# Folding the squares of W_out with VectorE before the norm products, and squaring at the end of a step

## The chip, the cores and the metric

The kernel runs on one core of one Trainium2 chip. The metric is device time in microseconds (us) of one execution. Five engines work side by side, each through its own queue in order: TensorE (PE in the profile, with its weight loads as PEld), VectorE (DVE), ScalarE (ACT), GpSimd (POOL) and SyncE (SP, which here only issues DMAs).

## The reference

Attention over a pooled memory is followed by one feed-forward layer. `phi` is softmaxed over 32 memory slots and pools `k` and `v` into 32 rows per head; the queries attend to these rows; the heads side by side are the rows of `x` (4608 x 512).

```python
a = softmax(phi, axis=2)
k_m = einsum('bhsm,bhsd->bhmd', a, k); v_m = einsum('bhsm,bhsd->bhmd', a, v)
attn = softmax(q @ k_m.T / 8, axis=-1)
x = (attn @ v_m) as (4608, 512)
h = x @ w_in            # 512 x 2048
g = h - tanh(h)
out = g @ w_out         # 2048 x 512
```

## The kernel before, in words

**Precision and the check.** `w_in` and `w_out` come as float64. The fast path splits each into two float16 parts (`win_hi`, `win_lo`, `wout_hi`, `wout_lo`) and uses a polynomial for `h - tanh(h)`. This is right only if the sizes of the inputs lie in certain windows, so the kernel also measures these: per column of W_out, the sum of squares must lie in `WO_WIN`. All measurements go into the tile `stat`; `check` (word GG, L948) compares them on VectorE, `check_all` (GX, L964) sums the verdicts with one TensorE product `pgood`, and if the sum falls short a slow path (`wide_path`) recomputes everything. With the inputs used it does not run.

**The steady part.** The tokens are cut into 18 units of 256 (u = 0 to 17), W_in's columns into four blocks of 512 (fb = 0 to 3). One step is one pair (u, fb); a loop at L896 walks over them from u = 4, and the table `PLAN_C` counts them by slots, slot = 4u + fb. The profile's names don't hold the pair; the order listings below do (`g142` is u = 14, fb = 2, slot 58). A step does, in program order:

- `mm1` (L562): 24 to 48 products into the one PSUM tile `hs`, from the attention weights `ah`, `al` and the tiles `ph`; then ScalarE squares it, `u<-hs` (L579).
- `g1` (L584): VectorE `h<-hs,u` (L587). After it `hs` may be written by the next step.
- the first words of the plan, among them `P` (L529): products into the PSUM tile `pp`, read by ScalarE (L537) and by VectorE in `PL` (L542).
- `g1_square` (L590, ScalarE), `a_forms` (L614: four VectorE adds `f<-g`, L621, of the step before), `g2` (L594: VectorE `h<-u,h`, L597).
- `mm2_blocks` (L686): 48 products of the step two before into PSUM tiles `x` and `o`.
- `window_sum` (L442, ScalarE), the plan's words after ";", `g2_high` (L600: ScalarE `g<-h`, L603) and `g3` (L606: GpSimd `g<-h,g`, L608).
- words put off (`due`): CE and CQ load blocks of the float64 weights, CW squares one on GpSimd (`fy<-chk`, L439), SI and SO square a quarter of the weights on ScalarE; then `evict` (L761) where a unit ends; then the plan's words after "|".

**The norms.** `squares_out` (SO, L468) lets ScalarE square four blocks of W_out (128 x 2048, float16) into `sqo`, which lies in the one buffer `e`. `norms_out` (NO, L472) multiplies it with a column of ones on TensorE: for each of four column groups four products that add up in PSUM, 16 in all, into the tile `pno`; ScalarE copies the sums out, `wn<-pno` (L483), and after the last part VectorE adds the four parts into `stat` (L486). For W_in there are SI and NI likewise; there, for three of four parts, `squares_sum` (SS, L449) has VectorE fold the four blocks into one first (two float16 adds, L452 and L453), and NI needs four products.

**One PSUM buffer, `pa`,** serves `pp`, `pno`, `pni`, the scores `psc`, the transposes `ptr` and `pgood` in turn: each waits until the one before has been read out.

**The order** on every engine is that in which the code issues the instructions (`in_order`, L938); no scheduler moves anything.

Of the kernel before, what the change touches and what calls it, by code (L numbers as in the profile page):

```python
# [18 lines left out]
P = 128  # L19
# [20 lines left out]
CW = (  # L40
    0.33333331252017, -0.13333128520786, 0.053934788850892, -0.021660115374759,
    0.0082189218977914, -0.0025104593252184, 0.000420695493864,
)
# [2 lines left out]

V_WIN = (2.0 ** -12, 0.0025)
WI_WIN = (1.002 * 2.0 ** -6, 1.497)
WO_WIN = (2.0 ** -6, 3.5)
N_F1 = 32  # L50
N_ROWS = 2

# [285 lines left out]
def split_path(ctx, tc, c, ins, out):  # L338
    nc = tc.nc
# [95 lines left out]
    def window(k):  # L435

        hf = raws.pop(k).bitcast(F32).rearrange("p (f w) -> p f w", w=2)[:, :, 1]
        y = big.tile([P, 512], F32, tag="ot", name=f"fy{k}")
        nc.gpsimd.tensor_tensor(y, hf, hf, op=ALU.mult)  # L439
        return y, k  # L440

    def window_sum(y, k):  # L442
        nc.scalar.activation(y, y, AF.Relu, bias=c["one"], scale=-(2.0 ** 30), accum_out=stat[:, k : k + 1])
# [28 lines left out]
    def norms_out(part):  # L472
        if part == 0:
            acc["n"] = big.tile([P, 4, 4], F32, tag="wn", name="wn", bufs=1)
        sq = acc.pop(("q", part))
        pa = ps_a.tile([P, 2, 512], F32, tag="pa", name=f"pno{part}")
        for k in range(4):
            for i in range(4):
                nc.tensor.matmul(
                    pa[:, 0, k : k + 1], sq[:, i, P * k : P * k + P], c["ones16"],  # L480
                    start=(i == 0), stop=(i == 3),
                )
        nc.scalar.activation(acc["n"][:, :, part], pa[:, 0, 0:4], AF.Copy, scale=(S_W * S_Q) ** -2)  # L483
        if part == 3:
            o = N_CHECK - 4
            nc.vector.tensor_reduce(stat[:, o : o + 4], acc["n"], axis=AX.X, op=ALU.add)  # L486
# [75 lines left out]
    def mm1(u, fb):  # L562
        hp = acc["hp"] if "hp" in acc else ps_h.tile([P, 4, UT], F32, tag="h", name=f"h{u}{fb}")
        for k in range(4):
            cs = slice(P * k, P * k + P)
            for b, ta, tu, w in segs(u):
                d = st[b]
                ph, pl = d["p"][fb][0:2]
                n = 0
                for g in range(2):  # L570
                    for px, ax in ((ph, "ah"), (ph, "al"), (pl, "ah")):
                        nc.tensor.matmul(  # L572
                            hp[:, k, tu : tu + w], px[:, g, cs], d[ax][:, g, ta : ta + w],
                            start=(n == 0), stop=(n == 5),
                        )
                        n += 1
        yield
        uu = big.tile([P, 4, UT], F32, tag="us" if "hp" in acc else "uu", name=f"u{u}{fb}", bufs=1 if "hp" in acc else 2)
        nc.scalar.activation(uu, hp, AF.Square, scale=1.0 / (S_A * S_P))  # L579
        gs[u, fb] = (hp, uu)  # L580
# [3 lines left out]
    def g1(u, fb, stay=False):  # L584
        hp, uu = gs[u, fb]
        h3 = hp if stay else big.tile([P, 4, UT], F32, tag="h3", name=f"h3{u}{fb}")
        nc.vector.scalar_tensor_tensor(h3, hp, C2 * S_G / (S_A * S_P), uu, op0=ALU.mult, op1=ALU.mult)  # L587
        gs[u, fb] = (h3, uu)

    def g1_square(u, fb):  # L590
        uu = gs[u, fb][1]
        nc.scalar.activation(uu, uu, AF.Square, bias=c["beta"])  # L592

    def g2(u, fb, stay=False):  # L594
        hp, uu = gs[u, fb]
        h3 = big.tile([P, 4, UT], F32, tag="h3", name=f"h3{u}{fb}") if stay else hp
        nc.vector.scalar_tensor_tensor(h3, uu, CC, hp, op0=ALU.add, op1=ALU.mult)  # L597
        gs[u, fb] = (h3, uu)

    def g2_high(u, fb):  # L600
        h3 = gs[u, fb][0]
        gg = big.tile([P, 2, 4, UT], F16, tag="gg", name=f"g{u}{fb}", bufs=3)
        nc.scalar.activation(gg[:, 0], h3, AF.Copy)  # L603
        gs[u, fb] = (h3, gg)

    def g3(u, fb, eng):  # L606
        h3, gg = gs[u, fb]
        eng.tensor_tensor(gg[:, 1], h3, gg[:, 0], op=ALU.subtract)  # L608

    def a_block(gg, th, kh):  # L610

        return gg[:, :, 2 * kh : 2 * kh + 2, P * th : P * th + P]

    def a_forms(u, fb):  # L614

        gg = gs[u, fb][1]
        a11, a21, a12, a22 = (a_block(gg, th, kh) for kh in range(2) for th in range(2))
        f = big.tile([P, 2, 4, 2, P], F16, tag="uu", name=f"f{u}{fb}")
        s4, s3, s1, s2 = (f[:, :, i] for i in range(4))
        for o, x, y, op in ((s3, a21, a11, ALU.subtract), (s1, a21, a22, ALU.add), (s2, s3, a22, ALU.add), (s4, a12, s2, ALU.subtract)):  # L620
            nc.vector.tensor_tensor(o, x, y, op=op)  # L621
        gs[u, fb] = (f, gg)
# [207 lines left out]
    def go(word, whole=True):  # L830

        name = word.rstrip("0123456789")
        run = going.pop(word, None) or STEPS[name](*(int(x) for x in word[len(name):]))
        if run is None or not hasattr(run, "send"):
            return
        for _ in run:
            if not whole:
                going[word] = run
                return

    for word in START.split():
        if ":" in word:
            k, tag = word.split(":")
# [17 lines left out]
    PLAN_C = (  # L861
# [5 lines left out]
    )  # L867
    tasks = {}
    for b in range(3, B):
# [4 lines left out]
    loads, chk, due, squared = list(range(32)), [], [], []  # L874

    def borrow(tag):
        chk.append(loads.pop(0))
        load_raw(chk[-1], tag, "chk")

    def step(word, late=False):  # L880
        if word[0] == "C" or word[:2] in ("SI", "SO"):
            if not late:
                due.append(word)
            elif word == "CW":
                squared.append(window(chk.pop(0)))
            elif word[0] == "C":
                borrow({"E": "e", "Q": "q", "S": "sc"}[word[1]])
            else:
                go(word)
        else:  # L890
            go(word)
# [4 lines left out]
    for sl, (u, fb) in enumerate(slots, 18):  # L896
        if sl == 18:
            acc["x"] = ps_h.tile([P, 2, 512], F32, tag="h", name="x")
            acc["hp"] = ps_h.tile([P, 4, UT], F32, tag="h", name="hs")
        todo = ["", "", ""]  # L900
        for w in tasks.get(sl, []):
            w, _, todo_2 = w.partition("|")
            w, _, todo_1 = w.partition(";")
            for i, x in enumerate((w, todo_1, todo_2)):
                todo[i] += " " + x

        def do(i):
            for x in todo[i].split():
                step(x)

        list(mm1(u, fb))
        g1(u, fb)
        do(0)
        g1_square(u, fb)
        a_forms(*forms.pop())
        g2(u, fb)
        queue.append((u, fb))
        v, vb = queue.pop(0)
        mm2_blocks(v, vb, vb == 0, vb == NFB - 1)
        while squared:  # L920
            window_sum(*squared.pop(0))
        do(1)
        g2_high(u, fb)
        g3(u, fb, nc.gpsimd)
        while due:
            step(due.pop(0), True)
        evict()
        forms.append((u, fb))
        do(2)
    a_forms(*forms.pop())  # L930
    for u, fb in queue:
        mm2_blocks(u, fb, fb == 0, fb == NFB - 1)
# [15 lines left out]
def check(tc, c, big):  # L948
# [4 lines left out]
    o = N_F1  # L953
    for n, (lo, hi) in ((2 * B, V_WIN), (DF // P, WI_WIN), (DM // P, WO_WIN)):
        s, g = stat[:, o : o + n], good[:, o : o + n]
# [196 lines left out]
```

## Time and profile before

| what | us |
|---|---|
| median of 3 runs (lowest, highest) | 660.62 (660.04, 660.83) |
| the profiled execution's own time | 660.87 |
| its span from first to last instruction | 659.1 |
| PE busy | 641.5 (97%) |
| DVE busy | 522.7 (79%) |
| ACT busy | 375.7 (57%) |
| POOL busy | 251.0 (38%) |

A row of the timeline holds start, duration, engine, line, operation, output and inputs, shape, and the number of instructions taken together; in brackets how long the engine stood idle before it, and what ended that. The chain of waits follows the last instruction back, at each step to what released it or to the instruction before it on its engine. A busy PE is not PE at its peak.

### The profile page before, as it was taken

How to read it: one execution, taken by the hardware profiler on the slowest of the kernel's cores; microseconds unless marked ns; L12 is line 12 of the kernel's file. 1: busy time of each engine (PE TensorE's matmuls, PEld its weight loads, DVE VectorE, ACT ScalarE, POOL GpSimd, SP SyncE). 2: the span in 40 equal slices, each digit the busy share in tenths (PEclk: the TensorE clock that was granted, in tenths of full speed). 3: DMA queues.
4: the chain of work that ended last, by engine and by line, in shares of the span. 5: the costliest groups of instructions: out<-in, count | busy, mean ns of one | idle time of the engine just before them, and what ended most of it. 6: DMA issues, size and time to landing. Idle time of an engine off the chain costs nothing.

```text
span 659.1 us, 15599 instructions
## 1 busy us (share of the span) xinstructions
PE 641.5 (97%) x6690; PEld 455.5 (69%) x6690; DVE 522.7 (79%) x790; ACT 375.7 (57%) x509; POOL 251.0 (38%) x173
## 2 busy tenths in 40 slices
PE   8879999999999999999999999999999999999996
PEld 4355656566557777777776777777687777887785
DVE  6989999999855787875988679767977686867763
ACT  4567686666424456545655465545654577666541
POOL 0315141221222245442535253625452455455521
PEclk9999999999999999999999999999999999999999
DMA  8999245302423402333331524141505333234201
GB/s 342 375 377 393 96 169 184 114 2 65 145 96 102 145 20 74 113 101 133 105 114 65 168 66 153 60 142 66 163 25 195 101 100 125 61 109 142 77 33 37
DMA packets 25996, 84.98 MB, mean 129 GB/s; under 512 B 2880, under 2 KB 2880, under 8 KB 25152
## 3 DMA queue, kind: packets, MB, share of 16 engines
q1 hardware_dynamic: 24624, 81.55, 36.1%
q10 hardware_dynamic: 1296, 2.36, 0.9%
q8 instruction: 54, 0.88, 0.6%
q14 instruction: 22, 0.18, 0.1%
HBM read 72.37 MB, written 11.53 MB: 127 GB/s over the span
## 4 chain that ended last, share of the span: by engine, by line
PE 76%; DVE 12%; DMA 6%; issue 2%; ACT 2%; POOL 1%; SPq 0%; DVEq 0%; ACTq 0%
PE hs L572 20%; PE x L715 13%; PE o L708 12%; PE o L715 10%; PE o L651 6%; PE h L572 4%; DMA kv<-in_kva_dram 3%; PE o1h L651 3%; PE pp L524 3%; PE pkv L220 2%; DMA raw<-in_w_out_dram 2%; DVE h L587 2%; DVE wt L384 1%; DVE h L597 1%; PE psc L272 1%
## 5 line engine op out<-in xcount | busy, mean ns | idle before, releaser
L608 POOL TENSOR_TENSOR g<-h,g 128x1024 f16<-128x1024 f32 x64 | 138.5, 2165 | 329.2 <-ACT g L603 234.3
L572 PEld LDWEIGHTS <-ph 128*128 128x128 f16 x2304 | 176.7, 98 | 20.7 <-issue 6.0
L572 PE MATMUL hs<-ah,ph 128*128 128x256 f16 (+3 forms) x1152 | 151.5, 246 | 0.0
L587 DVE SCALAR_TENSOR_TENSOR h<-hs,u 128x1024 f32<-128x1024 f32 x54 | 65.9, 1220 | 91.3 <-ACT u L579 91.2
L603 ACT ACTIVATE g<-h 128x1024 f16<-128x1024 f32 x72 | 75.9, 1055 | 91.7 <-DVE h L597 89.5
L572 PE MATMUL hs<-al,ph 128*128 128x256 f16 (+3 forms) x576 | 127.6, 246 | 0.0
L592 ACT ACTIVATE u<-u,beta 128x1024 f32<-128x1024 f32 x72 | 82.4, 1147 | 55.1 <-DVE h L587 54.1
L708 PE MATMUL o<-wout_hi,g 128*128 128x512 f16 x432 | 104.7, 380 | 0.0
L715 PEld LDWEIGHTS <-f 128*128 128x128 f16 x896 | 87.5, 98 | 10.3
L597 DVE SCALAR_TENSOR_TENSOR h<-u,h 128x1024 f32<-128x1024 f32 x72 | 87.4, 1216 | 0.8 <-ACT u L592 0.7
L579 ACT ACTIVATE u<-hs 128x1024 f32<-128x1024 f32 x54 | 55.0, 1019 | 55.3 <-PE hs L572 50.8
L715 PE MATMUL x<-bt,f 128*128 128x256 f16 x672 | 82.5, 273 | 0.0
L715 PEld LDWEIGHTS <-g 128*128 128x128 f16 x672 | 64.1, 98 | 26.6 <-issue 5.0
L708 PEld LDWEIGHTS <-g 128*128 128x128 f16 x432 | 40.5, 98 | 44.0 <-issue 8.1
L651 PEld LDWEIGHTS <-g 128*128 128x128 f16 x384 | 36.6, 98 | 46.6 <-issue 3.4
L621 DVE TENSOR_TENSOR f<-g 128x512 f16<-128x512 f16 x112 | 64.9, 620 | 4.3 <-POOL g L608 3.4
L651 PE MATMUL o<-wout_hi,g 128*128 128x512 f16 x192 | 58.8, 380 | 0.0
L572 PE MATMUL h<-ah,ph 128*128 128x256 f16 (+3 forms) x384 | 49.6, 246 | 0.1
L572 PE MATMUL h<-al,ph 128*128 128x256 f16 (+2 forms) x192 | 42.4, 246 | 0.2 <-POOL al L515 0.2
L542 DVE SCALAR_TENSOR_TENSOR ph<-pp,ph 128x1024 f16<-128x1024 f32 x31 | 37.6, 1213 | 0.6 <-ACT ph L537 0.6
L537 ACT ACTIVATE ph<-pp 128x1024 f16<-128x1024 f32 x32 | 32.5, 1017 | 7.4 <-PE pp L524 7.4
L651 PE MATMUL o<-wout_lo,g 128*128 128x512 f16 x96 | 36.4, 379 | 0.0
(146 smaller groups left out, 979.1 us busy)
## 6 DMA issues: line engine op xcount, KB each, us to landing
kv<-in_kva_dram SPq DMA_DIRECT2D x20, 516.0 KB, 4.2
q<-in_qt_dram SPq DMA_DIRECT2D x16, 576.0 KB, 4.3
chk<-in_w_in_dram SPq DMA_DIRECT2D x16, 512.0 KB, 5.6
chk<-in_w_out_dram SPq DMA_DIRECT2D x16, 512.0 KB, 3.4
out_dram<-r SPq DMA_DIRECT2D x27, 256.0 KB, 2.4
kv<-in_kva_dram SPq DMA_DIRECT2D x6, 1032.0 KB, 9.0
raws<-in_w_in_dram SPq DMA_DIRECT2D x12, 512.0 KB, 7.2
raw<-in_w_out_dram SPq DMA_DIRECT2D x12, 512.0 KB, 6.6
```

The lines of the kernel that those rows point to most:

```text
L542: nc.vector.scalar_tensor_tensor(pl, pa, S_P / (S_V * S_W), ph, op0=ALU.mult, op1=ALU.subtract)
L572: nc.tensor.matmul(hp[:, k, tu : tu + w], px[:, g, cs], d[ax][:, g, ta : ta + w], start=(n == 0), stop=(n == 5),)
L579: nc.scalar.activation(uu, hp, AF.Square, scale=1.0 / (S_A * S_P))
L587: nc.vector.scalar_tensor_tensor(h3, hp, C2 * S_G / (S_A * S_P), uu, op0=ALU.mult, op1=ALU.mult)
L592: nc.scalar.activation(uu, uu, AF.Square, bias=c["beta"])
L597: nc.vector.scalar_tensor_tensor(h3, uu, CC, hp, op0=ALU.add, op1=ALU.mult)
L603: nc.scalar.activation(gg[:, 0], h3, AF.Copy)
L608: eng.tensor_tensor(gg[:, 1], h3, gg[:, 0], op=ALU.subtract)
L621: nc.vector.tensor_tensor(o, x, y, op=op)
L651: nc.tensor.matmul(o, gx[:, k, P * tt : P * tt + P], wx[:, 4 * fb + k, :], start=(first and k == 0 and wx is wout_hi and gx is gh), stop=( ...
L708: nc.tensor.matmul(o[th], gg[:, 0, k, P * th : P * th + P], wout_hi[:, 4 * fb + k, :], start=(first and k == 0), stop=False)
L715: nc.tensor.matmul(dst, a(1 - n, kk), b(n, kk), start=(new and kk == 0 and n == 0), stop=(end and kk == 1 and n == 1))
```

## The change

Between the squaring of a part of W_out and its norm products stands now a step word SS, that is, the two VectorE adds of `squares_sum`; `norms_out` makes four products in place of sixteen. The words move in the plan: SO0 stays at slot 56, SO1 to SO3 stand at 59, 61 and 63 (before 58, 60, 62), each right behind the NO of the part before it; NO0 to NO3 at 59, 61, 63 and 65 (before 57, 59, 61, 63); SS0 to SS3 at 58, 60, 62 and 64. And in every step the words SI and SO come after `evict` and after the words behind "|", instead of before both. The window of W_out's norms is a little narrower.

```diff
-WO_WIN = (2.0 ** -6, 3.5)
+WO_WIN = (1.002 * 2.0 ** -6, 3.493)
...
-            for i in range(4):
-                nc.tensor.matmul(
-                    pa[:, 0, k : k + 1], sq[:, i, P * k : P * k + P], c["ones16"],
-                    start=(i == 0), stop=(i == 3),
-                )
+            nc.tensor.matmul(pa[:, 0, k : k + 1], sq[:, 0, P * k : P * k + P], c["ones16"], start=True, stop=True)
...
-        ... (56, "CW CW CQ CQ SO0"), (57, "CW CW CQ CQ | NO0"), (58, "CW CQ SO1"),
+        ... (56, "CW CW CQ CQ SO0"), (57, "CW CW CQ CQ"), (58, "CW CQ ; SS0"),
...
-        while due:
+        while due and due[0][0] == "C":
             step(due.pop(0), True)
         evict()
         forms.append((u, fb))
         do(2)
+        while due:
+            step(due.pop(0), True)
```

On ScalarE at the end of slot 54 stood before (`sqi3` is the square of W_in's last quarter; `kT7` and `vh7` are copies out of the transposes `ptr7`, which the scores of batch 7 and VectorE's `vl` need; `u133` opens the elementwise work of the next step):

```order
L603 ACTIVATE g132_6779<-h3132_6699 128x1024
L447 ACTIVATE sqi3_6786<-win_hi_97 128x2048
L264 ACTIVATE kT7_6793<-ptr7_6788 128x128
L496 ACTIVATE vh7_6795<-ptr7_6788 128x128
L579 ACTIVATE u133_6847<-hs_2449 128x1024
```

At the same place stands now:

```order
L599 ACTIVATE g132_6779<-h3132_6699 128x1024
L264 ACTIVATE kT7_6791<-ptr7_6786 128x128
L492 ACTIVATE vh7_6793<-ptr7_6786 128x128
L447 ACTIVATE sqi3_6797<-win_hi_97 128x2048
L575 ACTIVATE u133_6847<-hs_2449 128x1024
```

The two copies have moved ahead of the square; `u133` is behind all three as before.

On ScalarE from slot 60 to the start of slot 62 stood before (`sqo2` is the square of W_out's third part, `pno2` its norm product's PSUM tile; `u152` opens slot 62's elementwise work):

```order
L603 ACTIVATE g150_7529<-h3150_7454 128x1024
L470 ACTIVATE sqo2_7536<-wout_hi_99 128x2048
L579 ACTIVATE u151_7591<-hs_2449 128x1024
L592 ACTIVATE u151_7591<-u151_7591,beta_62 128x1024
L753 ACTIVATE r140_7602<-x_2448 128x256
L754 ACTIVATE r141_7603<-x_2448 128x256
L443 ACTIVATE fy20_7532,stat_67<-fy20_7532,one_61 128x512
L603 ACTIVATE g151_7643<-h3151_7593 128x1024
L483 ACTIVATE wn_7139<-pno2_7658 128x4
L579 ACTIVATE u152_7724<-hs_2449 128x1024
```

At the same place stands now:

```order
L599 ACTIVATE g150_7503<-h3150_7426 128x1024
L575 ACTIVATE u151_7563<-hs_2449 128x1024
L588 ACTIVATE u151_7563<-u151_7563,beta_62 128x1024
L749 ACTIVATE r140_7574<-x_2448 128x256
L750 ACTIVATE r141_7575<-x_2448 128x256
L443 ACTIVATE fy20_7506,stat_67<-fy20_7506,one_61 128x512
L599 ACTIVATE g151_7615<-h3151_7565 128x1024
L479 ACTIVATE wn_7367<-pno1_7630 128x4
L470 ACTIVATE sqo2_7636<-wout_hi_99 128x2048
L575 ACTIVATE u152_7686<-hs_2449 128x1024
```

The square has moved from ahead of `u151` to ahead of `u152`, behind the copy `wn`, which is now that of part 1. Parts 1 and 3 have moved in the same way, from ahead of `u143` and `u153` to ahead of `u150` and `u160`.

On VectorE at the turn from slot 58 to 59 stood before (`af7` is batch 7's transposed attention weights, `h3143` slot 59's first elementwise product):

```order
L597 SCALAR_TENSOR_TENSOR h3142_7184<-u142_7182,h3142_7184 128x1024
L320 STREAM_TRANSPOSE af7_7261<-sc7_6862 128x576
L587 SCALAR_TENSOR_TENSOR h3143_7298<-hs_2449,u143_7296 128x1024
L542 SCALAR_TENSOR_TENSOR ph71_7329<-pp71_7304,ph71_7329 128x1024
L621 TENSOR_TENSOR f142_7333<-g142_7263 128x2x256 x2
```

At the same place stands now:

```order
L593 SCALAR_TENSOR_TENSOR h3142_7165<-u142_7163,h3142_7165 128x1024
L320 STREAM_TRANSPOSE af7_7242<-sc7_6862 128x576
L452 TENSOR_TENSOR sqo0_7041<-sqo0_7041 128x1024
L453 TENSOR_TENSOR sqo0_7041<-sqo0_7041 128x512
L583 SCALAR_TENSOR_TENSOR h3143_7279<-hs_2449,u143_7277 128x1024
```

The two adds stand between the transpose and the next step's first product. SS2, at the turn from slot 62 to 63, stands in the same way behind a transpose; SS1 and SS3 stand directly behind the step's `h<-u,h`.

6 rows, old and new, of the table PLAN_C are left out of this document.

## The prediction

> **What bounds the kernel now.** I read the busy shares first, then PE's waits in the stretch that the change touches, then the chain of waits. The page's busy shares, and PE's own waits, asked from 500 to 606 us and from 590 us to the end:
>
> ```profile
> PE 641.5 (97%) x6690; PEld 455.5 (69%) x6690; DVE 522.7 (79%) x790; ACT 375.7 (57%) x509; POOL 251.0 (38%) x173
> ...
> PE psc L272 <- DVE vl L498: 0.7, 1, 0.7
> ...
> PE pgood L967 <- DVE grow L960: 0.4, 1, 0.4
> ```
>
> PE looks like the bound: in some 150 us it waits twice, for 0.7 and 0.4 us. But the second wait says that the other engines came later than PE there. The chain of waits, in order of time:
>
> ```profile
> 591.56 2.63 PE hs L572 x24
> ...
> 594.27 1.03 ACT u L579
> ...
> 596.55 2.36 DVE f L621 x3
> ...
> 624.21 0.04 issue
> 624.25 0.38 PE pgood L967 x2
> ```
>
> From 594 to 624 us the end is set by a loop of elementwise work: GpSimd's `g`, VectorE's `f` and `h`, ScalarE's `g`, GpSimd's next `g`. Its period is seen in GpSimd's starts, PE's in the starts of `hs` (timeline):
>
> ```profile
> 593.98 2.13 POOL L608 TENSOR_TENSOR g<-h,g 128x1024 f16<-128x1024 f32 x1 [3.44 <-issue]
> 601.72 2.23 POOL L608 TENSOR_TENSOR g<-h,g 128x1024 f16<-128x1024 f32 x1 [3.44 <-issue]
> ...
> 606.22 0.27 PE L572 MATMUL hs<-ah,ph 128*128 128x256 f16 x1
> ...
> 613.62 0.27 PE L572 MATMUL hs<-ah,ph 128*128 128x256 f16 x1
> ```
>
> 7.74 us against 7.40: over these slots (64 to 68) the loop has nothing to give back, and whatever it is late by at slot 64 it is late by at `pgood`. So there are two paths nearly level, PE's and the loop's, and they meet at 624.25 us with the loop 0.45 us behind. Behind it PE runs to the end without a wait. The time after is 660.87 us (the profiled execution; 0.25 above the median of 660.62) plus the loop's shift there, unless PE is later still.
>
> **PE's part.** Sixteen and four norm products, each with the row that follows on PE:
>
> ```profile
> 551.18 0.54 PE L479 MATMUL pno<-ones,sqo 128*128 128x1 f16 x16
> 551.59 0.24 PE L572 MATMUL hs<-ah,ph 128*128 128x192 f16 x1
> ...
> 320.83 0.24 PE L461 MATMUL pni<-ones,sqi 128*128 128x1 f16 x4
> 320.94 0.27 PE L715 MATMUL x<-wout_hi,g 128*128 128x256 f16 x1
> ```
>
> 551.59 - 551.18 = 0.41 us becomes 0.11: four times 0.30 = 1.20 us. Slot 54's `psc` wait (0.67) goes: it waited for `vl`, `vl` for `vh`, `vh` for `sqi3`, and `vh` now runs 1.8 us earlier. What is late there next is nothing on PE; `u133` still stands behind `sqi3`, so the loop gets that gain only at slot 56, and there VectorE's `f` waits for a GpSimd piece that did not move:
>
> ```profile
> 523.18 1.16 POOL L302 TENSOR_TENSOR sc<-sc,sm 128x576 f32<-128x576 f32 x1
> 524.44 0.72 DVE L621 TENSOR_TENSOR f<-g 128x512 f16<-128x512 f16 x2
> ```
>
> It ends at 524.34. By the rule found below the first `f` then ends at 524.62 at the earliest and the second half of 0.72 later, 524.98 instead of 525.16: between 0 and 0.67 I take -0.2 for the loop. Together PE could be 0.67 + 1.20 = 1.87 us earlier. SI and SO issue no DMA, and SP's and GpSimd's instructions keep their order.
>
> **What a VectorE add costs beside GpSimd.** Small adds that wait show in these rows:
>
> ```profile
> 318.56 0.69 DVE L452 TENSOR_TENSOR sqi<-sqi 128x1024 f16<-128x1024 f16 x1
> 319.28 0.43 DVE L453 TENSOR_TENSOR sqi<-sqi 128x512 f16<-128x512 f16 x1
> 319.87 2.12 POOL L608 TENSOR_TENSOR g<-h,g 128x1024 f16<-128x1024 f32 x1 [4.13 <-issue]
> 320.41 1.62 DVE L312 TENSOR_SCALAR sz<-sz 128x18 f32<-128x18 f32 x1
> ...
> 611.65 2.23 POOL L439 TENSOR_TENSOR fy<-chk 128x512 f32<-128x512 f32 x2
> 611.74 2.42 DVE L621 TENSOR_TENSOR f<-g 128x512 f16<-128x512 f16 x2
> ```
>
> The folding adds take 0.69 and 0.43 where GpSimd stands still. An 18-element operation started under GpSimd's `g` ends with it (1.62 us, at 322.03), and `f` ends at 614.16, 0.28 behind GpSimd's 613.88: a VectorE operation of this kind waits for the GpSimd instruction that is running. The Trainium skill, page "SBUF — State Buffer", section "Who interferes with whom", states it as a lock: a VectorE instruction with two SBUF inputs and a GpSimd instruction that reads SBUF exclude each other for a whole instruction, and issue order decides. The trace agrees with it (the 1.62 us above). It speaks against SS0 and SS2; if VectorE did not wait, the sum below would be +1.2 instead of +1.4, since other work binds soon after.
>
> **The loop, slot by slot** (times in the frame of before; minus is earlier). The rows of slots 58 to 60:
>
> ```profile
> 543.87 0.77 DVE L320 STREAM_TRANSPOSE af<-sc 128x576 f32<-128x576 f32 x1
> 544.95 1.89 ACT L470 ACTIVATE sqo<-wout_hi 128x2048 f16<-128x2048 f16 x1
> 545.12 2.14 POOL L608 TENSOR_TENSOR g<-h,g 128x1024 f16<-128x1024 f32 x1 [3.72 <-ACT g L603]
> 546.75 1.00 ACT L579 ACTIVATE u<-hs 128x1024 f32<-128x1024 f32 x1
> 547.79 1.23 DVE L587 SCALAR_TENSOR_TENSOR h<-hs,u 128x1024 f32<-128x1024 f32 x1 [3.15 <-ACT u L579]
> 549.27 1.23 DVE L542 SCALAR_TENSOR_TENSOR ph<-pp,ph 128x1024 f16<-128x1024 f32 x1 [0.26 <-ACT ph L537]
> ...
> 554.09 0.16 ACT L483 ACTIVATE wn<-pno 128x4 f32<-128x4 f32 x1
> 554.36 0.41 PE L524 MATMUL pp<-win_hi,vh 64*32 64x512 f16 x8
> 554.52 1.02 ACT L579 ACTIVATE u<-hs 128x1024 f32<-128x1024 f32 x1 [0.27 <-PE hs L572]
> 557.40 1.16 POOL L302 TENSOR_TENSOR sc<-sc,sm 128x576 f32<-128x576 f32 x1
> 557.85 1.33 DVE L621 TENSOR_TENSOR f<-g 128x512 f16<-128x512 f16 x2
> ```
>
> *Slot 58.* `sqo1` leaves its place ahead of `u143`. But SS0 comes behind the transpose: the first add runs from 544.56 to 545.25, GpSimd's `g` is due at 545.12 and waits 0.1, the second add waits until 547.4 and ends 0.28 later. `h` can start at 547.6 instead of 547.79; with the -0.2 from before, -0.4. VectorE also stood 0.26 for ScalarE's `ph`, late because of `u`; that now comes in time: -0.7 at the end of the step.
>
> *Slot 59.* `sqo1` now stands behind `g` and `wn`. `wn` comes at 554.09 - 0.7 = 553.4, `sqo1` 0.1 later, and `u` follows its start by 546.75 - 544.95 = 1.80: 555.3 instead of 554.52, +0.8. Part of this is covered: `f` waited for GpSimd's subtraction before (1.33 for two where 0.72 stands above), and that is 0.7 earlier now. `f` starts at 557.85 + 0.8 and takes 0.72: 559.37 against 559.18, about +0.15. `pp` on PE wants to start at 554.36 - 0.67 - 0.41 - 0.30 = 552.98, but shares `pa` with `pno`, which `wn` reads until 553.5: PE loses 0.55 of its lead. SS1 ends before GpSimd's `g`; what follows it is hidden by GpSimd's three pieces in slot 61. The loop goes on at +0.15.
>
> The rows of slot 62, and two of 63 and 64:
>
> ```profile
> 570.12 0.16 ACT L483 ACTIVATE wn<-pno 128x4 f32<-128x4 f32 x1
> 570.56 0.41 PE L524 MATMUL pp<-win_hi,vh 64*32 64x512 f16 x8
> 571.78 1.23 DVE L587 SCALAR_TENSOR_TENSOR h<-hs,u 128x1024 f32<-128x1024 f32 x1
> ...
> 581.19 1.28 POOL L515 TENSOR_TENSOR al<-af,ah 128x576 f16<-128x576 f32 x1 [0.15 <-ACT ah L513]
> ...
> 583.99 0.27 PE L572 MATMUL hs<-ah,ph 128*128 128x256 f16 x1
> ```
>
> *Slot 62.* `wn` at 570.25, `sqo2` at 570.35, `u` 1.80 later at 572.15, `h` 1.04 behind it (547.79 - 546.75) at 573.2 instead of 571.78: **+1.4**. GpSimd has little to do in this slot that could hide it. PE's `pp` again waits for `wn`, until 570.45 against 570.56: PE's lead is down to 0.1.
>
> *Slots 63 to 65.* SS2's second add waits for `g` as SS0's did, but GpSimd's `al` (581.19 + 1.28 before) is late by 1.5 anyway and holds `f`: nothing more. PE needs `al` for `hs` at 583.99; 582.47 + 1.5 = 583.97, so PE's last 0.4 of lead (0.1 and pno2's 0.30) goes. `sqo3` delays `u160`, but there VectorE's `f` waits for two `fy` of GpSimd in any case. SS3 fits ahead of GpSimd's `g`; `wn` of part 3 and the reduction into `stat`, now in slot 65, stand ahead of an `f` that waits for `fy`, and cost nothing while it does (0.2 if not). The loop stays at +1.4, and keeps it to `pgood`, 625.65.
>
> **Sum:** -0.2 (slot 56) - 0.5 (58) + 0.85 (59) + 1.25 (62) = +1.4 us. 660.87 + 1.4 = 662.27, on the median's footing **662.0**. Bounds: if the second adds get ahead of GpSimd (in slot 58 they are due within 0.05 us of each other) and the 0.67 reaches the loop whole, +0.8; if each is held for a second GpSimd instruction, 1.1 more (half of the 2.23 above) at SS0 and at SS2, about half of it hidden behind GpSimd's work: up to +2.4. So 661.4 to 663.0.
>
> **Rivals.** *PE is the bound after all, faster.* For it: 97% busy, 1.1 us of waits. Then 0.67 + 1.20 = 1.87 us come through: 658.75. It decides if ScalarE's `wn` in slot 62 comes 1.5 us earlier than in before, so that `pp` keeps its lead, and `grow` too. Against it: before, `wn` ends 0.11 us ahead of `pp` in slot 60 and 0.28 in slot 62, so PE has no room to run ahead of ScalarE. 0.14. *Gains and losses cancel.* The loop finds cover for `sqo2` that I do not see, and arrives between -1.0 and +0.8: 659.6 to 661.4, middle 660.6. 0.21. *The adds are held by several GpSimd instructions in a row*, because GpSimd's next one is already queued each time: +2.4 or more, 663.0 to 663.6. 0.05. My forecast has 0.60; its upper two thirds are slower by over 0.2% (above 661.94), 0.41, the rest, 0.19, within. 0.2%, 1.3 us, is about what a measurement can tell from no change here.
>
> Faster 0.14, within 0.21 + 0.19 = 0.40, slower 0.41 + 0.05 = 0.46. The range leaves out the first and the third rival, 0.19 together: 659.6 to 663.0.
>
> **What would show it.** Right: `psc` has no wait; the first `wn` near 553.4 and `pp` right behind it; `u` in slot 62 some 2.9 us behind ScalarE's `g`; the second add of SS0 and SS2 over 1.5 us long; PE waiting about 1 us or more at `pgood`. Wrong: a `pgood` wait under 0.5 us with `hs` of slot 64 more than 1 us earlier (PE bounds), or second adds of 0.43 us.

## The result, and the profile after

The changed kernel takes 662.62 us (median of 22 runs, 661.04 to 664.63) where the kernel before takes 661.0 us (median of 22 runs beside it): a ratio of 1.002, 95% interval 1.001 to 1.0029. It is slower by 0.7 to 1.9 us, about as much as one can just tell from no change. Forecast were 662.0 us, and 1.4 us more than before. The forecast started from the median of three runs of the kernel before, 660.62 us; the median of its 22 runs is 661.0, and that is 0.4 of the 0.6 us between 662.0 and 662.62. One of the twelve executions of p_fold, an experiment below, took 1103.13 us at a granted clock of 0.56; its median of 660.01 us counts it, its ratio leaves it out.

First the page's busy shares, then PE's waits from 480 us to 661 us, in the kernel after:

```profile
PE 641.7 (97%) x6642; PEld 456.1 (69%) x6642; DVE 531.1 (80%) x798; ACT 374.8 (57%) x509; POOL 251.1 (38%) x173
...
PE pp L520 <- ACT wn L479: 1.3, 2, 0.9
PE x L711 <- DVE r L765: 1.1, 1, 1.1
PE pkv L220 <- DMA kv<-in_kva_dram: 0.8, 1, 0.8
PE pgood L965 <- DVE grow L958: 0.5, 1, 0.5
PE hs L568 <- DVE h L583: 0.2, 1, 0.2
```

PE has 48 instructions fewer, and VectorE, with eight more, is busy 8.4 us longer, though the adds' own time is 4 x 1.1 us: VectorE's busy time contains time in which it is held. The wait for `vl` is gone. In its place PE waits 1.3 us for ScalarE's `wn`, 1.1 us at an `x` in slot 66 for VectorE's evict (`r`, which reads the `x` before it), and 0.5 us at `pgood`.

**Where the time came.** The profiled executions can't be laid over each other from their starts: after is 2.40 us later already at the end of slot 54, ahead of everything that the change moves. I therefore measure both from ScalarE's `g` of slot 54 and call the way from there to `pgood` the stretch. Before (timeline, ScalarE's `g` of slots 54 and 59, and `pgood` on PE):

```profile
509.25 1.06 ACT L603 ACTIVATE g<-h 128x1024 f16<-128x1024 f32 x1 [1.96 <-DVE h L597]
...
553.13 1.06 ACT L603 ACTIVATE g<-h 128x1024 f16<-128x1024 f32 x1 [2.15 <-DVE h L597]
...
624.25 0.38 PE L967 MATMUL pgood<-grow,ones 128*128 128x1 f32 x2 [0.45 <-DVE grow L960]
```

And after, the same three:

```profile
511.65 1.06 ACT L599 ACTIVATE g<-h 128x1024 f16<-128x1024 f32 x1 [1.96 <-DVE h L593]
...
554.61 1.06 ACT L599 ACTIVATE g<-h 128x1024 f16<-128x1024 f32 x1 [1.88 <-DVE h L593]
...
628.03 0.35 PE L965 MATMUL pgood<-grow,ones 128*128 128x1 f32 x2 [0.54 <-DVE grow L958]
```

The stretch was 624.25 - 509.25 = 115.00 us and is 628.03 - 511.65 = 116.38 us: **+1.38**. Behind `pgood` both kernels take the same 34.8 us to the end. The table shows by how much ScalarE's `g` at the end of a slot starts later (plus) than before, from this origin; in slot 59, for example, (554.61 - 511.65) - (553.13 - 509.25) = -0.92. The tables are worked out from unrounded times, so the last digit can differ by one from what the rows give.

| kernel | slot 56 | 58 | 59 | 60 | 61 | 62 | 63 | 64 | 68 | `pgood` |
|---|---|---|---|---|---|---|---|---|---|---|
| forecast | -0.2 | -0.2 | -0.7 | +0.15 | +0.15 | +1.4 | +1.4 | +1.4 | +1.4 | +1.4 |
| after | -0.20 | -0.22 | -0.92 | -0.08 | -0.08 | +1.16 | +1.13 | +1.28 | +1.28 | +1.38 |

The whole loss comes in two steps, from slot 59 to 60 (+0.84) and from 61 to 62 (+1.24). These are the rows of the second on ScalarE (timeline of after):

```profile
571.47 1.06 ACT L599 ACTIVATE g<-h 128x1024 f16<-128x1024 f32 x1 [0.85 <-DVE h L593]
572.44 0.16 ACT L479 ACTIVATE wn<-pno 128x4 f32<-128x4 f32 x1
572.49 1.90 ACT L470 ACTIVATE sqo<-wout_hi 128x2048 f16<-128x2048 f16 x1
574.29 1.02 ACT L575 ACTIVATE u<-hs 128x1024 f32<-128x1024 f32 x1
```

`u` of slot 62 starts 2.82 us behind the start of `g`, and 1.80 of that is the square. The chain of waits shows that it counts: in the kernel after it runs from 539.5 us to `pgood` almost wholly through the elementwise engines, with the squares of the second, third and fourth part, the adds of SS1 and both held adds as pieces of its own; among them are:

```profile
547.43 2.28 DVE sqo L453
...
555.58 0.16 ACT wn L479
555.74 1.79 ACT sqo L470
557.53 0.93 ACT u L575
...
572.60 1.80 ACT sqo L470
574.39 0.93 ACT u L575
...
581.59 2.28 DVE sqo L453
...
628.03 0.35 PE pgood L965 x2
```

Before, the chain changed to the loop only at 594 us; from 513 us up to there it ran on PE. The second add of SS0, on VectorE, and GpSimd's `g` beside it (timeline):

```profile
546.75 0.65 DVE L452 TENSOR_TENSOR sqo<-sqo 128x1024 f16<-128x1024 f16 x1
547.43 2.28 DVE L453 TENSOR_TENSOR sqo<-sqo 128x512 f16<-128x512 f16 x1
549.64 1.21 DVE L583 SCALAR_TENSOR_TENSOR h<-hs,u 128x1024 f32<-128x1024 f32 x1
...
547.31 2.13 POOL L604 TENSOR_TENSOR g<-h,g 128x1024 f16<-128x1024 f32 x1 [3.72 <-ACT g L599]
```

GpSimd's `g` started 0.12 us ahead of the add and ended at 549.44; the add, 0.43 us of work, ended at 549.71, 0.27 behind it. SS2's second add took 2.28 us too; SS1's and SS3's, which stand directly behind the step's `h`, took 0.42.

### The profile page after: what moved, and what is told of

Same layout as the page of the kernel before. It is cut to its first block, busy times and chain, and to the rows that moved or that the text cites. A ratio compares the mean times of both kernels' runs of the same rounds, so it can differ in the third digit from the quotient of the medians.

```text
span 662.9 us, 15516 instructions
## 1 busy us (share of the span) xinstructions
PE 641.7 (97%) x6642; PEld 456.1 (69%) x6642; DVE 531.1 (80%) x798; ACT 374.8 (57%) x509; POOL 251.1 (38%) x173
## 4 chain that ended last, share of the span: by engine, by line
PE 78%; DVE 11%; DMA 3%; issue 3%; ACT 2%; POOL 2%; ACTq 0%; SPq 0%; DVEq 0%; POOLq 0%
PE hs L568 17%; PE x L711 12%; PE o L704 11%; PE o L647 9%; PE o L711 8%; PE h L568 6%; PE o1h L647 3%; PE pp L520 3%; DVE f L617 3%; PE pkv L220 2%; DMA kv<-in_kva_dram 2%; DVE h L593 2%; PE warm L785 1%; DVE h L583 1%; PE psc L272 1%
```

## The experiments

The theory: the elementwise loop sets the time from about slot 58 on; what the change costs is the squares in odd slots, where nothing covers them, and the two held adds; what it saves on PE (1.87 us) is not on the path. The rival: PE sets the time, so the products and PE's waits are what counts. All kernels are timed in five rounds beside the kernel before, whose median was 660.9 to 661.2 us on these occasions; the stretch is that of the profiled execution.

| kernel | us | ratio to before (95%) | stretch | against before |
|---|---|---|---|---|
| before | 661.0 | 1 | 115.00 | |
| after | 662.62 | 1.002 (1.001 to 1.0029) | 116.38 | +1.38 |
| b_four | 660.34 | 0.9991 (0.998 to 1.0002) | 114.89 | -0.11 |
| b_late | 660.42 | 0.9997 (0.9984 to 1.001) | 114.72 | -0.28 |
| a_sixteen | 662.49 | 1.0019 (1.0007 to 1.003) | 116.35 | +1.35 |
| a_no2 | 660.72 | 1.0003 (0.9987 to 1.0018) | 115.03 | +0.03 |
| a_noadd | 661.43 | 1.0001 (0.9989 to 1.0013) | 115.54 | +0.54 |
| a_early | 667.38 | 1.0087 (1.0073 to 1.0101) | 122.84 | +7.84 |
| a_first | 661.68 | 1.0011 (0.9999 to 1.0022) | 115.71 | +0.71 |
| p_cover | 659.84 | 0.9978 (0.9966 to 0.999) | 114.15 | -0.85 |
| p_fold | 660.01 | 0.9979 (0.9965 to 0.9992) | 114.00 | -1.00 |
| p_fold_ca | 659.32 | 0.9969 (0.9958 to 0.998) | 113.25 | -1.75 |

Most differences are near what the timing can tell, so where a slot is in question I go by the trace, one execution of each kernel; its shifts at slots 56 and 57 agree within 0.03 us between the kernels that have the squares last in a step. b_four, a_sixteen, a_no2 and a_noadd leave blocks out of the sums or count them twice, so in these the window of W_out's norms is 0 to 1000, and the slow path stays out.

### One part alone, or undone

**b_four**: the kernel before with four norm products.

```
-            for i in range(4):
-                nc.tensor.matmul(
-                    pa[:, 0, k : k + 1], sq[:, i, P * k : P * k + P], c["ones16"],
-                    start=(i == 0), stop=(i == 3),
-                )
+            nc.tensor.matmul(pa[:, 0, k : k + 1], sq[:, 0, P * k : P * k + P], c["ones16"], start=True, stop=True)
```

> The kernel before with four norm products per part of W_out in place of sixteen, nothing else moved; three of the four blocks' squares are left out of the sum. TensorE has 48 products less, 1.2 us by the rows. Theory (the loop of elementwise work sets the time, TensorE only fills it): the stretch from ScalarE's g at the end of slot 54 to pgood stays at 114.9 to 115.0 us (before 115.00), TensorE waits about 1 us more, at pp and pgood; the time is that of before within 0.3 us. Rival (TensorE is the bound): the stretch is 113.8 and the time 1.2 us shorter.

The products shrank as costed (timeline of b_four, PE, the four and what follows them):

```profile
552.24 0.24 PE L478 MATMUL pno<-ones,sqo 128*128 128x1 f16 x4
552.34 0.24 PE L568 MATMUL hs<-ah,ph 128*128 128x192 f16 x1
```

0.10 us instead of 0.41, four times; yet the stretch is 0.11 shorter, not 1.2. PE's waits in the same kernel say where the rest went:

```profile
PE psc L272 <- DVE vl L494: 0.7, 1, 0.7
PE pgood L963 <- DVE grow L956: 0.4, 1, 0.4
PE pp L520 <- ACT wn L479: 0.4, 1, 0.4
PE x L711 <- DVE r L765: 0.3, 1, 0.3
```

`psc` and `pgood` waited before as well; the two waits of 0.4 and 0.3 are new. PE came early and was stopped by ScalarE and VectorE. That speaks for the theory; with the rival it would have been 113.8. The time alone doesn't decide it: 1.2 us less would be a ratio of 0.9982, just inside the interval.

**b_late**: the kernel before with the squares last in a step.

```
-        while due:
+        while due and due[0][0] == "C":
             step(due.pop(0), True)
         evict()
         forms.append((u, fb))
         do(2)
+        while due:
+            step(due.pop(0), True)
```

> The kernel before with the one edit that the squares come last in a step. Theory: the wait of the scores in slot 54/55 (0.67 us) goes, but the loop gets only about 0.2 of it: the stretch from slot 54 to pgood is 114.8 us, the time 0.2 us shorter, not to be told from before. Rival (TensorE is the bound): stretch 114.3, time 0.67 us shorter.

The wait for `vl` was gone, and the loop had -0.21 of it at slot 56 and -0.29 at slot 68: of 0.67 us on PE less than half came through. The theory holds; the rival had 114.3.

**a_sixteen**: the changed kernel with sixteen products, after the adds.

```
-            nc.tensor.matmul(pa[:, 0, k : k + 1], sq[:, 0, P * k : P * k + P], c["ones16"], start=True, stop=True)
+            for i in range(4):
+                nc.tensor.matmul(
+                    pa[:, 0, k : k + 1], sq[:, i, P * k : P * k + P], c["ones16"],
+                    start=(i == 0), stop=(i == 3),
+                )
```

> The kernel after with sixteen norm products per part again, each block after the adds, so the sum counts blocks twice; TensorE has its 1.2 us back, the adds stay. Theory: the stretch stays at 116.4 us as in after (at most 0.15 more), the time too. Rival (TensorE is the bound): 117.6 and 1.2 us longer than after. Rival (the adds on VectorE are the loss): 116.4 as well.

116.35 against 116.38: the 1.2 us of PE work cost nothing. PE's wait for `wn` fell from 1.3 to 0.6 us and that at `x` from 1.1 to 0.8. With b_four this settles that PE's saving is off the path, before the change and after it.

**a_no2**: the changed kernel without the square of W_out's third part.

```
     def squares_out(part):
+        if part == 2:
+            acc["q", part] = acc["q1"]
+            return
...
         nc.scalar.activation(acc["q", part], wout_hi[:, 4 * part : 4 * part + 4, :], AF.Square, scale=S_Q)
+        acc["q%d" % part] = acc["q", part]
```

> The kernel after without the square of W_out's third part: the adds and products of that part run on the tile of the second part once more. Only 1.9 us of ScalarE's work at the turn from slot 61 to 62 is gone. Theory: h of slot 62 starts right behind evict, 1.2 us earlier than in after, and all of it reaches pgood: stretch 115.1 to 115.3, the time that of before or up to 0.3 above. Rivals (TensorE is the bound; the adds are the loss): 116.4 and the time of after.

ScalarE at the turn to slot 62 (timeline of a_no2):

```profile
568.60 1.06 ACT L603 ACTIVATE g<-h 128x1024 f16<-128x1024 f32 x1 [0.85 <-DVE h L597]
569.56 0.16 ACT L483 ACTIVATE wn<-pno 128x4 f32<-128x4 f32 x1
569.61 1.02 ACT L579 ACTIVATE u<-hs 128x1024 f32<-128x1024 f32 x1
```

`u` comes 1.01 us behind `g` instead of 2.82. Up to slot 61 the shifts are those of after; slot 62 is at -0.19 instead of +1.16, and `pgood` at +0.03 instead of +1.38. The 1.35 us are as much as the whole loss, which doesn't make the square its only cause: the square takes back what the change had gained ahead of it (-0.08 at slot 61), and the adds' cost is in the rest.

### The adds, and what holds them

**a_noadd**: the changed kernel without the eight adds for W_out (`added` starts as {3}, the one part of W_in that is not folded).

```
+    added = {3}
+
     def squares_sum(i):
         sq = acc["q", i]
+        if i in added:
+            return
+        added.add(i)
```

> The kernel after without the eight VectorE adds for W_out; the four products take one block's squares, three are left out. Theory (ScalarE's square at the turn from slot 61 to 62 is the loss, the adds are mostly hidden): h of slots 59 and 63 comes 1.5 us earlier than in after, but GpSimd's al holds f soon after, so the stretch from slot 54 to pgood is 115.7 to 116.1 us (before 115.00, after 116.38). Rival (the adds waiting for GpSimd are the loss): 115.0 or below, the time of before.

115.54: the adds cost 0.84 us of the stretch, more than the 0.3 to 0.7 that I had put on them; my expectation was missed by 0.16. By slots, without them: -1.28 instead of -0.92 at slot 59 (SS0, 0.36), a further gain of 0.15 from slot 60 to 61 where with SS1 there is none, and from slot 62 to 63 the loop gains 0.35 where with SS2 it gains 0.03. Is that the adds' own work, or the hold?

**a_early**: SS0 and SS2 at the end of slots 57 and 63, behind `h` as SS1 and SS3 are.

```
-        ... (57, "CW CW CQ CQ"), (58, "CW CQ ; SS0"),
+        ... (57, "CW CW CQ CQ ; SS0"), (58, "CW CQ"),
...
-        ... (62, "CW CQ ; SS2"), (63, "CW CW CQ CQ SO3 | NO2"),
+        ... (62, "CW CQ"), (63, "CW CW CQ CQ SO3 ; SS2 | NO2"),
```

> The changed kernel with all its instructions; only the adds SS0 and SS2 stand elsewhere: SS0 at the end of slot 57 and SS2 at the end of slot 63, each directly behind the step's last h product, with no transpose between (as SS1 and SS3 stand already), so that the second add is done before GpSimd's g starts. The theory: what the adds cost the loop is mostly that the second one is held by GpSimd's running g (2.28 us instead of 0.43, twice), so both second adds take about 0.43 here, slot 59 is entered at about -1.28 against the kernel before (without any adds it was -1.28, with them -0.92), slot 61 keeps SS1's 0.14, and slots 62 and 63 come to +0.8 and about +0.5: the stretch up to the verdicts' product is 115.6 to 115.8 us, 0.6 to 0.8 below the changed kernel's 116.38. The rival: it is the adds' own 1.1 us on VectorE, wherever they stand, and the hold lies beside other work; then the stretch stays at 116.2 to 116.4.

A clear miss: 122.84 us. Both second adds did take 0.43, but I had not looked at what stands behind them. VectorE at the end of slot 57 (timeline of a_early), and GpSimd beside it:

```profile
536.39 0.43 DVE L453 TENSOR_TENSOR sqo<-sqo 128x512 f16<-128x512 f16 x1
536.74 0.42 DVE L764 SCALAR_TENSOR_TENSOR r<-x,r 128x256 f32<-128x256 f32 x1
537.19 0.42 DVE L765 SCALAR_TENSOR_TENSOR r<-x,r 128x256 f32<-128x256 f32 x1
537.53 1.81 DVE L766 TENSOR_TENSOR r<-r,r 128x256 f32<-128x256 f32 x1
539.26 1.25 DVE L769 TENSOR_TENSOR r<-r 128x256 f32<-128x256 f32 x1
...
536.93 2.13 POOL L604 TENSOR_TENSOR g<-h,g 128x1024 f16<-128x1024 f32 x1 [3.38 <-ACT g L599]
539.01 2.40 POOL L439 TENSOR_TENSOR fy<-chk 128x512 f32<-128x512 f32 x2
```

Slot 57 ends a unit, and evict stands behind the adds. In the kernel after, with no adds there, its two `TENSOR_TENSOR` (L766, L769) take 0.41 and 0.42 us and are both under way before GpSimd's `g` starts; here the first is held by `g` and the second by a `fy`. Slot 58 is at +2.59 instead of -0.22: evict starts 1.07 us later for the adds' own time, and its two held operations take 2.23 us longer. The larger loss, 3.76 us from slot 63 to 64, begins on PE, whose product of part 2 was now directly behind SS2 (timeline of a_early, PE, that product and the first and the last row of the 24 products of `hs` behind it):

```profile
589.42 0.27 PE L478 MATMUL pno<-ones,sqo 128*128 128x1 f16 x4 [3.50 <-DVE sqo L453]
589.56 0.37 PE L568 MATMUL hs<-ah,ph 128*128 128x256 f16 x1
...
594.42 0.42 PE L568 MATMUL hs<-ah,ph 128*128 128x256 f16 x1
```

PE takes its instructions in order, and `hs` of the next step stood behind this wait. And behind it PE was slow: from the start of the first of the 24 products to that of the last are 594.42 - 589.56 = 4.86 us, in the kernel after 2.51, and the granted clock is 0.50 from 589.4 to 595.0 us, where it was 1.00 from 584 to 586. So the run didn't separate the adds' work from the hold. It did show the hold go from one operation to the next.

**a_first**: the same question without evict and without a moved product: in slots 58 and 62 the adds stand ahead of the transpose instead of behind it, and nothing else changes.

```
-        tasks.setdefault(sl, []).append(words)
+        tasks.setdefault(sl, []).insert(0 if sl in (58, 62) else 99, words)
```

> The changed kernel with all its instructions; only, in slots 58 and 62, VectorE does the adds SS0 and SS2 ahead of the transpose instead of behind it, so that both adds (0.65 + 0.43 us) can end before GpSimd's g starts; no other engine's order changes, and evict, which stands in slots 57 and 61, is not behind them. The theory: the adds cost the loop through the hold by GpSimd's g, not through their own length. Then both second adds take 0.43, the transpose (one input) runs beside g, h of slot 59 starts when u is ready (about 1.45 us earlier than in the changed kernel), slot 59 is entered at -1.28 instead of -0.92, slot 61 keeps SS1's 0.14, slot 62 is at about +0.8 and slot 63 on at +0.45 to +0.6; the stretch up to the verdicts' product is 115.6 to 115.8 us, the time 0.6 to 0.8 below the changed kernel's. The rival: the adds' own time on VectorE is what counts; then the stretch stays at 116.2 to 116.4. A third way: the transpose is now held by g as the add was; then nothing is gained or the stretch grows (116.4 or more).

VectorE at the turn from slot 58 to 59, and GpSimd's `g` (timeline of a_first):

```profile
543.87 0.69 DVE L452 TENSOR_TENSOR sqo<-sqo 128x1024 f16<-128x1024 f16 x1
544.59 0.42 DVE L453 TENSOR_TENSOR sqo<-sqo 128x512 f16<-128x512 f16 x1
544.93 0.77 DVE L320 STREAM_TRANSPOSE af<-sc 128x576 f32<-128x576 f32 x1
545.99 1.22 DVE L583 SCALAR_TENSOR_TENSOR h<-hs,u 128x1024 f32<-128x1024 f32 x1 [0.28 <-ACT u L575]
...
545.12 2.14 POOL L604 TENSOR_TENSOR g<-h,g 128x1024 f16<-128x1024 f32 x1 [3.72 <-ACT g L599]
```

The add takes 0.42, the transpose runs its usual 0.77 us beside `g`, and VectorE even stands 0.28 for `u`. Slot 59 is at -1.27, slot 61 at -0.42, slot 62 at +0.81, slot 63 at +0.46, the stretch is 115.71: as expected in every slot. So of the adds' 0.84 us the hold is 116.38 - 115.71 = 0.67 and the rest, 0.17, is SS1's 0.15 at slot 61 and little else. The expected 0.6 to 0.8 us are in the trace; the timing agrees (1.0011 against 1.002) but can't show it by itself.

### Versions that follow from it

If the squares' place is what costs, they belong where the loop has cover: at the end of even slots, ahead of slots in which GpSimd has several pieces to do. **p_cover** leaves the adds and the four products out of the change and keeps the rest, with SO1 to SO3 at slots 60, 62 and 64, one later than after has them:

```
-        ... (58, "CW CQ ; SS0"), (59, "CW CQ SO1 | NO0"), (60, "CW CQ ; SS1"), (61, "CW CQ SO2 | NO1"), (62, "CW CQ ; SS2"),
+        ... (58, "CW CQ"), (59, "CW CQ | NO0"), (60, "CW CQ SO1"), (61, "CW CQ | NO1"), (62, "CW CQ SO2"),
...
-        (63, "CW CW CQ CQ SO3 | NO2"), (64, "CW CW CQ CQ ; SS3"), (65, "CW CW CQ CQ | NO3"),
+        (63, "CW CW CQ CQ | NO2"), (64, "CW CW CQ CQ SO3"), (65, "CW CW CQ CQ | NO3"),
```

> Squares last in a step, sixteen products and no adds as in before, and the squares and products moved: SO1 to SO3 at slots 60, 62, 64, NO0 to NO3 at 59, 61, 63, 65. Theory: no square stands any more where nothing covers it (slot 58 of before, 61 of after), and GpSimd's long slots cover all of them: the loop gains 0.2 at slot 56 and 0.9 at slot 59, stretch 113.9 us, the time 1.1 us shorter than before. Rival (TensorE is the bound): only the wait of the scores goes, 114.3.

-0.85: faster than before (0.9978) and a little less than expected. Slot 59 is at -1.27 and slot 64 still at -1.15; about 0.3 is lost at slot 65, behind SO3.

**p_fold** has the adds and four products as well, each SS where neither a transpose nor evict follows, and each NO in the slot behind its SS; the third part's square goes into another buffer (`sc`):

```
+        (59, 'CW CQ ; SS0'), (60, 'CW CQ SO1 | NO0'), (61, 'CW CQ'), (62, 'CW CQ SO2'),
+        (63, 'CW CW CQ CQ ; SS1'), (64, 'CW CW CQ CQ SO3 ; SS2 | NO1'), (65, 'CW CW CQ CQ | NO2'),
+        (66, 'CW CW CQ ; SS3'), (67, 'CW | NO3'),
```

> The same places for the squares with the adds and four products: SS0 to SS3 at slots 59, 63, 64, 66, each directly behind the step's h, so that they end before GpSimd starts; NO0 to NO3 at 60, 64, 65, 67, the third part's tile in the buffer of the scores. Theory: 113.9 us as p_cover, the 48 products less make no difference, since pgood waits for the loop. Rival (TensorE is the bound): 113.1, the wait of the scores and 1.2 us less.

-1.00, as expected: with their places right the adds cost nothing that the stretch shows, and against p_cover the 1.2 us that PE saves bring 0.15 in the stretch and nothing that can be timed.

**p_fold_ca** is p_fold with three of GpSimd's window squares (`fy`, one each in slots 63, 65 and 66) done by ScalarE, since VectorE's `f` waits for GpSimd there:

```
+        if act:
+            nc.scalar.activation(y, hf, AF.Square)
+        else:
+            nc.gpsimd.tensor_tensor(y, hf, hf, op=ALU.mult)
```

> p_fold with one of the two window squares of slots 63, 65 and 66 on ScalarE instead of GpSimd. Theory: the loop's period falls from 7.74 us to 7.4 or less in the slots behind them, the loop reaches pgood before TensorE does, pgood no longer waits and TensorE's lead comes through: stretch 112.8 to 113.4, the time 1.6 to 2.2 us shorter than before. If the loop is bound by something other than the two window squares, 113.9 as p_fold.

-1.75 in the stretch, 659.32 us, ratio 0.9969: the lowest time of all, though its interval overlaps those of p_cover and p_fold; it is 0.2 to 0.4% below before, and with the kernel after at 1.002 below that too. The expected end of the wait at `pgood` did not come. The window square needs a block of the float64 weights that a DMA loads, and on ScalarE it now stands ahead of the next step's `u` (timelines of p_fold_ca, ScalarE behind slots 65 and 66, then PE):

```profile
600.32 0.69 ACT L440 ACTIVATE fy<-chk 128x512 f32<-128x512 f32 x1 [0.80 <-DMA chk<-in_w_out_dram]
...
608.59 0.68 ACT L440 ACTIVATE fy<-chk 128x512 f32<-128x512 f32 x1 [1.68 <-DMA chk<-in_w_out_dram]
609.18 1.00 ACT L578 ACTIVATE u<-hs 128x1024 f32<-128x1024 f32 x1
...
622.28 0.35 PE L995 MATMUL pgood<-grow,ones 128*128 128x1 f32 x2 [0.61 <-DVE grow L988]
```

The loop was at -2.23 in slot 64, at -1.85 in slot 65 behind SO3's square, at -2.31 in slot 66, and from slot 67 on, behind the wait of 1.68 us, at -1.85 again. Its period was 7.39 us from slot 65 to 66 and 8.21 from 66 to 67. PE stands 0.61 us at `pgood` for it. So the elementwise loop still ends last there, even in the fastest kernel, and the chain of waits goes through the second load (603.25 to 608.51 us): what SO3's square had cost was made up by slot 66, and the last loss is ScalarE's wait for the load. That an earlier load would end the wait at `pgood` is not shown.

## Why the prediction was right, step by step

**What bounds.** Right. PE at 97% was not the bound over the stretch: b_four and a_sixteen move 1.2 us of PE's work and the stretch by 0.11 and 0.03. The loop's shift at `pgood` came out as the change in the time.

**The sum.** Forecast -0.2, -0.5, +0.85, +1.25; measured -0.20 (slot 56), -0.72 (up to slot 59), +0.84 (slot 60) and +1.24 (slot 62), and two small terms that the sum did not have, +0.12 at slot 64 and +0.10 on the last way to `pgood`. Only the second was off by more than 0.15: `h` of slot 59 started 0.55 us earlier instead of 0.4, and behind it another 0.37 went instead of 0.3. Of the 0.15, 0.14 is GpSimd's `g`, which I had wait 0.1 us for the end of the first add: it started 1.14 us behind the start of ScalarE's `g`, 1.13 in the kernel before, while the first add was still running, and took its usual 2.13. The +0.12 at slot 64 (-0.03 at slot 63, +0.15 behind it) is SO3's square, which I had put at nothing because VectorE's `f` waits for two `fy` there. It does, but `u` of slot 64, counted from ScalarE's `g` of slot 63, comes 0.99 us later than in the kernel before, and the two `f` that waited get only 0.83 shorter (1.76 us before, 0.93 after). From slot 63 to 64 each of the five kernels with SO3 in slot 63 and SS2 in slot 62 or left out (after, a_sixteen, a_no2, a_noadd, a_first) loses 0.15, and b_four and b_late, with SO3 in slot 62, lose nothing. That the 0.22 too little in one term is as much as the two missing terms together, so that the sum came within 0.02 us, is luck.

**What a held add costs** was mis-sized, and this is the step that failed: "if VectorE did not wait, the sum below would be +1.2 instead of +1.4, since other work binds soon after". a_first, in which it does not wait, has +0.71: the hold is worth 0.67 us, not 0.2. For SS0 no other work bound soon after: the gain is kept whole (-1.27 at slot 59, and +0.84 behind it in either kernel). For SS2 I wrote that GpSimd's `al`, late anyway, holds `f`, "nothing more". But without the hold the loop gains back 0.35 us from slot 62 to 63. I had left that gain out of my sum and the hold's price with it, and the two errors cancel: that 1.4 was right there is luck.

**The rule itself** was right. A `TENSOR_TENSOR` of VectorE with both inputs in SBUF waits for the GpSimd instruction that is running; the held adds, `f` and evict's first `TENSOR_TENSOR` end 0.27 to 0.28 us behind it. The 1.62 us that the prediction gives beside the lock are a weaker witness: that row is a `TENSOR_SCALAR` with one tensor as its input (`sz<-sz`), and it ends 0.04 behind GpSimd's `g` (322.03 against 321.99). It was held, but it is not an instruction with two SBUF inputs, and the 0.28 is not the same for every operation. The Trainium skill, page "SBUF — State Buffer", section "Who interferes with whom", also says that a VectorE instruction with at most one SBUF input, outside the two-port modes, does not contend. The rows agree: in a_early `r<-x,r`, whose `x` lies in PSUM, takes 0.42 us beside `g` while `r<-r,r` takes 1.81, and in a_first the transpose takes 0.77 us beside `g`.

**The signs.** `psc` has no wait. The first `wn` stands at 555.58 - 2.40 = 553.18 (forecast 553.4) and `pp` right behind it, after a wait of 0.41. `u` of slot 62 comes 2.82 us behind `g` (2.9). The second adds of SS0 and SS2 take 2.28 us (over 1.5). Wrong was where PE's lost lead shows: I had it wait about 1 us or more at `pgood`; it waits 1.1 us in slot 66 already, where `x` is free only when evict has read it, and 0.5 at `pgood`. The evict is part of the loop's path and comes earlier in program order than `pgood`; I had followed only the chain that led to `pgood`.

**The rivals.** "PE is the bound after all" is refuted by b_four and a_sixteen. "Gains and losses cancel" did not come about, but was near: a_no2, the change without one square, does just that (+0.03). "Held by several GpSimd instructions in a row" did not happen: each held add in the changed kernel waited for one. Two operations in a row were held in a_early, where they took 2.23 us longer.

Not settled: the +0.10 between slot 68's `g` and `pgood`, which every kernel with the new places of the words has (a_early 0.40) and b_four and b_late have not. It lies behind the loop: VectorE's `grow` starts 0.95 to 0.96 us behind that `g` in both kernels, and `pgood` starts 0.27 behind the start of `grow` before and 0.37 after. Also open is what the loop could still gain if SO3 were covered, or if the loads came earlier in p_fold_ca, which I did not try.

## What to carry to other kernels

A busy engine is the bound only where its waits say so: look at which wait ends last at the point where the paths meet, and count an operation by what stands behind it in its queue. A small VectorE operation with both inputs in SBUF was cheap here only where it was done before GpSimd's next instruction started; moved by one place it took five times its length, and moved ahead of others of its kind it handed the hold on to them. Work that is put off to the end of a step goes to a step whose next start is held by something else. Work that is moved to another engine brings its own waits along: what it needs must be there when its new place in the queue comes up.

## What the hardware showed that I had not expected

- Of two adds in a row on VectorE, with GpSimd becoming ready during the first, GpSimd went ahead of the second, both times (SS0 and SS2 of the kernel after): the second took 2.28 us, and 0.42 where GpSimd was not yet ready.
- The hold counts as busy time of VectorE: the four pairs of adds are 4.4 us of work, and VectorE's busy time grew by 8.4.
- The sixteen norm products with their weight loads take 0.41 us, 26 ns each, and four 0.10 to 0.11; so per part two adds of 1.1 us on VectorE replaced 0.30 us of PE's work.
- Towards the end of PE's wait of 3.50 us in a_early the granted clock fell to 0.50 and stayed there to about 595.4 us, and from the first to the last of 24 products it took 4.86 us instead of 2.51. No other run has so long a wait of PE, or a clock below 1.00, between slot 54 and `pgood`; whether the wait is the cause no run here shows by itself.
